# The carried state's product, put on two column tiles of TensorE

## The chip, the cores and the metric

The kernel runs on one core of a Trainium2 chip. The metric is the device time of one execution in microseconds (us); less is better.

## What is computed

Two blocks, one after the other: a gated linear recurrence over 768 steps with a complex decay (4 batches, 8 heads, head size 48), and a feed-forward block with SiLU on its result, 3072 tokens of 384 numbers, 2048 hidden.

```python
mag = np.sqrt(a_re * a_re + a_im * a_im)
scale = np.minimum(mag, 0.999) / (mag + 1e-06)
a_re_n, a_im_n = (a_re * scale, a_im * scale)
for t in range(S):
    new_re = ar * S_re - ai * S_im          # ar, ai: the gates of step t
    new_im = ar * S_im + ai * S_re
    kv = np.einsum('bhd,bhe->bhde', k[:, :, t], v[:, :, t])
    S_re, S_im = (new_re + kv, new_im)
    y[:, :, t] = np.einsum('bhd,bhde->bhe', q[:, :, t], S_re)
x = y.transpose(0, 2, 1, 3).reshape(B * S, H * D)
h = x @ w_in
out = (h / (1 + np.exp(-h))) @ w_out
```

All inputs and outputs are float32 on the device; w_in and w_out come as 64-bit floats and are converted in the kernel.

## The kernel before

**Tiling.** Time is cut into chunks of C = 128 steps: 6 chunks in each of 4 batches, N = 24 in all, taken in pairs (p = 0 to 11). A chunk's complex decay is folded into its keys and queries: from the logarithm of the magnitude and from the angle, both summed over the chunk with one product each (`sums`, L343, tile `L`; `phases`, L322, tile `phase`), come the factors by which `rotated` (L366 to L370) multiplies k and q. The results `kr` and `qr` have, for each head, 2 x 48 = 96 columns (D2), the cosine half and the sine half.

**A chunk's attention.** `turned` puts kr and qr with their 96 columns on partitions (tile `T`; by TensorE, L386, for the first eight chunks, by DVE and DMAs for the others). `weights` (L406, tiles `a` and `w`) multiplies keys and queries of each head, and DVE masks the result (L411). `state` (L455, tile `s` in PSUM, 96 partitions of 8 x 48 numbers) multiplies, for each head, kr as the stationary operand (128 steps x 96 columns) by v as the moving one (128 steps x 48): the chunk's contribution to the carried state. DVE adds the old state and multiplies by the decay (L460 to L463, tile `S`); the next chunk of the same batch, two pairs later, reads it. The last chunk of a batch has no `state`, so it is called 20 times. `output` (L427 from v and `w`, L430 from the state and `T`, tile `y`) writes head pairs: the even head to PSUM partitions from 0 on, the odd one to those from 64 on. ACT copies `y` to `xT` (L436, L440), and small DMAs on SP's queue (L444) move a part of it.

**The feed-forward block.** For a pair of chunks (256 tokens) `hidden` (L473, tile `h`) makes two blocks of 128 hidden units per call, ACT applies SiLU (L243, tile `g`), and `result` (L485, tile `o`) adds their products with w_out. There are eight calls of each for a pair.

**Order.** TensorE's order is written out by hand throughout. From the fourth pair on, all engines' order is: a string names the parts, for the usual pair

```python
usual = ("c h h E kA qA L F h kB h tA G r qB r h tB r th h A X r h r aA pA sA yA h pB aB S r lA "
         "sB yB r lB D r")
```

where `h` and `r` are calls of `hidden` and `result` for the pair before, and `aA pA sA yA` are `weights` of chunk A, `phases` of the next pair, `state` and `output`. A `state` thus stands after `phases` or `sums` and is followed by `output`. Before that, `attend(n)` calls `weights` twice, `state` and `output`. Across the engines, semaphores that the framework sets keep the order; the products of one `state` signal once, after the last of them.

Of the kernel before, what the change touches and what calls it, by code (L numbers as in the profile page):

```python
# [55 lines left out]
def kernel(  # L56
# [19 lines left out]
    nc = tc.nc  # L76
# [6 lines left out]
    D2 = 2 * D  # L83
# [27 lines left out]
    def place(n):  # L111
        p, i = divmod(n, 2)
        c, half = divmod(p, B // 2)
        return 2 * half + i, c
# [333 lines left out]
    def state(n):  # L448

        x = X[n]  # L450
        if place(n)[1] == NCH - 1:
            return
        ps = p_m.tile([D2, H, D], F32, tag="m", name=f"s{n}")
        for h in range(H):
            nc.tensor.matmul(ps[:, h], lhsT=x["kr"][:, h].rearrange("p c d -> p (c d)"),  # L455
                             rhs=x["v"][:, h], start=True, stop=True)
        new = att.tile([D2, H, D], F32, tag="S", name=f"S{n + B}", bufs=5)
        by = decs[:, n].unsqueeze(2).to_broadcast([D2, H, D])
        if "S" in x:
            nc.vector.tensor_tensor(out=new, in0=ps, in1=x["S"], op=ALU.add)  # L460
            nc.vector.tensor_tensor(out=new, in0=new, in1=by, op=ALU.mult)
        else:
            nc.vector.tensor_tensor(out=new, in0=ps, in1=by, op=ALU.mult)  # L463
        X[n + B]["S"] = new
# [34 lines left out]
    def step(p, h, r, order):  # L499
# [3 lines left out]
        if p < NP:  # L503
            what["E"] = lambda: (table("exp"), both(decays, p))
            for i, x in enumerate("AB"):
                n = 2 * p + i
                what["k" + x] = lambda n=n: rotated(n, "k")
                what["q" + x] = lambda n=n: rotated(n, "q")
                what["t" + x] = lambda n=n: turned(n)
                what["a" + x] = lambda n=n: (weights(n, 0), weights(n, 1))  # L510
                what["s" + x] = lambda n=n: state(n)
                what["y" + x] = lambda n=n: output(n)
# [38 lines left out]
    def attend(n):  # L551
        weights(n, 0)
        weights(n, 1)
        state(n)
        output(n)
# [300 lines left out]
```

## Time and profile before

| | |
|---|---|
| time, median of 3 runs (lowest to highest) | 721.26 us (719.17 to 721.49) |
| profiled execution: its time | 722.11 us |
| profiled execution: span from first to last instruction | 720.4 us |
| granted TensorE clock, mean | 0.991 |
| TensorE matmuls, busy | 673.2 us, 3552 passes |
| TensorE weight loads, busy | 512.2 us, 3552 loads |
| VectorE (DVE), ScalarE (ACT) busy | 334.3 us, 362.8 us |

The profile names engines PE (TensorE's matmuls), PEld (its weight loads, which overlap matmuls), DVE, ACT, POOL and SP. A row of the groups reads: line, engine, operation, what is written and read, shapes, how often; then busy time, mean length of one in ns, and the idle time just before, with what ended it. For a matmul the first shape is rows times columns of the array that are in use, the second the moving operand. Ends of matmuls are modelled, since they are pipelined; starts are what distances are taken from. In the forty slices a digit is the busy share of 18 us in tenths.

### The profile page before, as it was taken

What the parts mean: (1) busy time and instruction counts of PE and PEld (TensorE: products, weight loads), DVE (VectorE), ACT (ScalarE), POOL (GpSimd) and SP (SyncE); (2) the same over time, 40 slices, a digit from 0 to 9 for tenths busy, and PEclk for the clock granted to TensorE, in tenths of its full rate; (3) what the DMA queues carried; (4) which work ended last, traced back from release to release, by engine and by line L of the source; (5) the groups of instructions that cost most, each with busy time, mean ns of one, the idle gap of its engine ahead of it and who ended that gap; (6) DMA issues with size and microseconds to landing.
All of it is one profiled execution on the core that took longest, in us unless ns stands there. A gap on an engine that the chain in (4) does not pass through costs nothing.

```text
span 720.4 us, 9485 instructions
## 1 busy us (share of the span) xinstructions
PE 673.2 (93%) x3552; PEld 512.2 (71%) x3552; DVE 334.3 (46%) x542; ACT 362.8 (50%) x597; POOL 59.7 (8%) x91
## 2 busy tenths in 40 slices
PE   0486997999999999999999999999999999999997
PEld 0275875777768778778778778777777777777774
DVE  4989758826443183182282272272272372151000
ACT  7985679548782382381381381381381481231201
POOL 2333001030000010010010010010010010010000
PEclk9998999999999999999999999999999999999999
DMA  9956347110150027128127228127227327023000
GB/s 184 232 133 159 93 135 175 45 45 17 48 97 1 28 41 139 47 34 142 51 37 138 52 34 143 50 33 134 60 29 125 73 27 128 28 40 51 29 1 25
DMA packets 207845, 55.51 MB, mean 77 GB/s; under 512 B 198424, under 2 KB 202672, under 8 KB 207792
## 3 DMA queue, kind: packets, MB, share of 16 engines
q1 hardware_dynamic: 199712, 43.55, 31.5%
q0 software_dynamic: 3584, 6.37, 4.4%
q10 hardware_dynamic: 4496, 4.92, 1.9%
q8 instruction: 30, 0.49, 0.3%
q14 instruction: 23, 0.19, 0.1%
HBM read 36.25 MB, written 4.76 MB: 57 GB/s over the span
## 4 chain that ended last, share of the span: by engine, by line
PE 86%; ACT 5%; DVE 3%; DMA 3%; SPq 2%; issue 1%; ACTq 0%
PE h L473 33%; PE o L485 32%; PE a L406 6%; PE s L455 4%; PE y L427 3%; PE y L430 2%; PE phase L322 2%; PE L L343 2%; PE tp L386 2%; DMA raw<-in_moe_w_in_dram 1%; ACT s L243 1%; ACT L238 1%; DMA q<-in_q_dram 1%; ACT mag L243 1%; SPq L135 1%
## 5 line engine op out<-in xcount | busy, mean ns | idle before, releaser
L473 PE MATMUL h<-xT,w 128*128 128x256 f32 x1152 | 261.2, 382 | 6.2 <-DMA xT<-y 6.2
L485 PE MATMUL o<-w,g 128*128 128x384 f32 x768 | 261.1, 488 | 0.0
L473 PEld LDWEIGHTS h<-xT,w 128*128 128x128 f32 x1152 | 219.5, 191 | 47.6 <-issue 8.1
L485 PEld LDWEIGHTS o<-w,g 128*128 128x128 f32 x768 | 144.2, 190 | 89.0 <-issue 2.2
L243 ACT ACTIVATE g<-h 128x512 f32<-128x512 f32 x96 | 56.3, 596 | 172.5 <-PE h L473 172.2
L411 DVE TENSOR_TENSOR w<-a,upto 128x512 f32<-128x512 f32 x48 | 33.0, 688 | 110.7 <-PE a L406 110.4
L436 ACT COPY xT<-y 128x384 f32<-128x384 f32 x24 | 11.5, 477 | 117.4 <-PE y L430 112.8
L357 POOL DMA_DIRECT2D decs<-ends x48 | 30.1, 633 | 465.1 <-DMA ends<-eq 464.5
L238 ACT ACT_TABLE_LOAD x50 | 64.2, 1283 | 2.2 <-PEq L840 1.3
L366 DVE TENSOR_TENSOR L<-k,L 128x384 f32<-128x384 f32 x24 | 13.3, 554 | 82.2 <-ACT L L243 82.2
L406 PEld LDWEIGHTS a<-T 96*128 96x128 f32 x384 | 46.7, 193 | 6.7 <-DVE w L411 1.0
L406 PE MATMUL a<-T 96*128 96x128 f32 x384 | 47.4, 276 | 0.8 <-DVE w L411 0.8
L322 PE MATMUL phase<-th,upto 128*128 128x384 f32 x48 | 22.0, 557 | 22.0 <-DVE th L301 19.4
L427 PE MATMUL y<-w,v 128*64 128x128 f32 (+1 forms) x384 | 39.6, 281 | 0.0
L346 DVE TENSOR_SCALAR L<-L 128x384 f32<-128x384 f32 x24 | 13.4, 557 | 56.2 <-PE L L343 55.9
L430 PE MATMUL y<-T,S 96*64 96x128 f32 x320 | 34.3, 273 | 0.0
L455 PEld LDWEIGHTS s<-v,kr 128*96 128x96 f32 x320 | 29.9, 165 | 4.9 <-issue 2.2
L324 DVE TENSOR_SCALAR turn<-phase 128x384 f32<-128x384 f32 x24 | 13.3, 556 | 42.3 <-PE phase L322 42.3
L491 ACT COPY ot<-o 128x384 f32<-128x384 f32 x24 | 11.5, 478 | 40.4 <-PE o L485 40.4
L243 ACT ACTIVATE mag<-mag 128x768 f32<-128x768 f32 (+1 forms) x39 | 30.6, 788 | 0.4
L243 ACT ACTIVATE s<-s 128x768 f32<-128x768 f32 (+1 forms) x39 | 30.5, 785 | 0.4
L455 PE MATMUL s<-v,kr 128*96 128x48 f32 x320 | 30.0, 247 | 0.2
(68 smaller groups left out, 617.5 us busy)
## 6 DMA issues: line engine op xcount, KB each, us to landing
T<-sq SPq DMA_DIRECT2D x192, 64.0 KB
raw<-in_moe_w_out_dram SPq DMA_DIRECT2D x16, 384.0 KB
raw<-in_moe_w_in_dram SPq DMA_DIRECT2D x24, 192.0 KB
out_dram<-ot ACTq DMA_DIRECT2D x24, 192.0 KB
re<-in_a_re_dram SPq DMA_DIRECT2D x18, 192.0 KB
k<-in_k_dram SPq DMA_DIRECT2D x18, 192.0 KB
q<-in_q_dram SPq DMA_DIRECT2D x18, 192.0 KB
im<-in_a_im_dram SPq DMA_DIRECT2D x17, 192.0 KB
```

Source lines behind the costliest of these rows:

```text
L238: chain(nc.scalar.preload_act_table_set({"exp": "natural_log_exp_and_others", "trig": "trig_and_small", "silu": "silu_and_others"}[of]))
L243: chain(nc.scalar.activation(out=out, in_=in_, func=func, **kw))
L322: nc.tensor.matmul(ps, lhsT=upto, rhs=th, start=True, stop=True)
L343: nc.tensor.matmul(ps, lhsT=half, rhs=cut(A[p]["l"], i), start=True, stop=True)
L357: nc.gpsimd.dma_start(out=decs[a * D:(a + 1) * D, n], in_=ends[n].rearrange("(h d) -> d h", d=D))
L406: nc.tensor.matmul(ps[:, h], lhsT=x["kT"][:, hh * HH + h], rhs=x["qT"][:, hh * HH + h], start=True, stop=True)
L411: nc.vector.tensor_tensor(out=x["w", hh], in0=ps, in1=upto.unsqueeze(1).to_broadcast([C, HH, C]), op=ALU.mult)
L427: nc.tensor.matmul(to, lhsT=v_[:, cols], rhs=x["w", h // HH][:, h % HH], start=True, stop=not carried)
L430: nc.tensor.matmul(to, lhsT=x["S"].rearrange("p h d -> p (h d)")[:, cols], rhs=x["qT"][:, h], start=False, stop=True)
L455: nc.tensor.matmul(ps[:, h], lhsT=x["kr"][:, h].rearrange("p c d -> p (c d)"), rhs=x["v"][:, h], start=True, stop=True)
L473: nc.tensor.matmul(ps[:, ji], lhsT=w1[:, dc, ts(jp * 2 + ji, C)], rhs=A[p]["xT"][:, dc], start=(dc == 0), stop=(dc == ND - 1))
L485: nc.tensor.matmul(A[p]["o"][m], lhsT=A[p]["g", jp][:, ji, ts(m, C)], rhs=w2[:, j], start=(j == 0), stop=(j == NJ - 1))
```

## The change

The stationary operand of each head's product, 96 columns, is cut in two: columns 0 to 63 and columns 64 to 95. Each part is a product of its own with the same moving operand, and writes its own partitions of the same PSUM tile (0 to 63, 64 to 95). For each head the wide part is issued first, then the narrow one. Nothing else is changed.

```diff
         ps = p_m.tile([D2, H, D], F32, tag="m", name=f"s{n}")
         for h in range(H):
-            nc.tensor.matmul(ps[:, h], lhsT=x["kr"][:, h].rearrange("p c d -> p (c d)"),
-                             rhs=x["v"][:, h], start=True, stop=True)
+
+            for m in (ds(0, 64), ds(64, D2 - 64)):
+                nc.tensor.matmul(ps[m, h], lhsT=x["kr"][:, h].rearrange("p c d -> p (c d)")[:, m],
+                                 rhs=x["v"][:, h], start=True, stop=True)
```

## The prediction

> **What bounds the kernel now.** I read the page first: busy time by engine, the forty slices, the chain that ended last.
>
> ```profile
> PE 673.2 (93%) x3552; PEld 512.2 (71%) x3552; DVE 334.3 (46%) x542; ACT 362.8 (50%) x597; POOL 59.7 (8%) x91
> ...
> PE   0486997999999999999999999999999999999997
> ...
> PE 86%; ACT 5%; DVE 3%; DMA 3%; SPq 2%; issue 1%; ACTq 0%
> PE h L473 33%; PE o L485 32%; PE a L406 6%; PE s L455 4%; PE y L427 3%; PE y L430 2%; PE phase L322 2%; PE L L343 2%; PE tp L386 2%; DMA raw<-in_moe_w_in_dram 1%; ACT s L243 1%; ACT L238 1%; DMA q<-in_q_dram 1%; ACT mag L243 1%; SPq L135 1%
> ```
>
> TensorE is full from slice 8 (126 us) to the end, and 86% of the chain is its work. The line that changes, L455, is 4% of the chain. The chain cut down to 40 to 66 us and to 70 to 90 us shows the four early calls of `state` on it too. So all twenty calls (24 chunks less the last one of each of four batches) lie on the path: a microsecond added to a call is one added to the end. Now the rows of the groups kept apart by shape:
>
> ```profile
> L406 PE MATMUL a<-T 96*128 96x128 f32 x384 | 47.4, 276 | 0.8 <-DVE w L411 0.8
> L427 PE MATMUL y<-w,v 128*64 128x128 f32 x336 | 38.5, 282 | 0.0
> ...
> L455 PE MATMUL s<-v,kr 128*96 128x48 f32 x320 | 30.0, 247 | 0.2
> ...
> L455 PEld LDWEIGHTS s<-v,kr 128*96 128x96 f32 x320 | 29.9, 165 | 4.9 <-issue 2.2 <-DVE w L411 0.6
> ```
>
> "128*96" is rows times columns of the array, "128x48" the moving operand. 320 is 20 calls x 8 heads x 2: each f32 product is two passes, each with its own weight load. The mean of 247 ns is a latency; what counts is the distance between starts, which the timeline of TensorE gives (start, length, group):
>
> ```profile
> 385.70 1.95 PE L406 MATMUL a<-T 96*128 96x128 f32 x16
> 387.49 0.81 PE L322 MATMUL phase<-th,upto 128*128 128x384 f32 x2
> 388.13 1.48 PE L455 MATMUL s<-v,kr 128*96 128x48 f32 x16
> 389.54 0.45 PE L427 MATMUL y<-w,v 128*64 128x128 f32 x4
> 389.81 0.40 PE L430 MATMUL y<-T,S 96*64 96x128 f32 x4
> ...
> 391.51 2.86 PE L473 MATMUL h<-xT,w 128*128 128x256 f32 x12
> ```
>
> From the starts: `phase` 0.64/2 = 0.32 us for a pass of 384 columns, so a pass streams at 384/320 = 1.2 columns per ns; `a` 1.79/16 = 112 ns for 128 columns (107 at that rate); `s` 1.41/16 = 88 ns for 48 columns, which at 1.2 stream in 40. So `s` isn't bound by its streaming but by its loads of 96 columns. `y`, from 389.54 to 391.51, has 32 passes of 128 columns in 1.97 us, 62 ns each, about half of 107: its heads alternate between PSUM partitions 0 and 64, that is between two column tiles, and these run side by side.
>
> What a change between whole-array and tiled work costs is seen at both ends of `y`, in narrow windows of the timeline:
>
> ```profile
> 389.37 0.25 PE L455 MATMUL s<-v,kr 128*96 128x48 f32 x1
> 389.54 0.45 PE L427 MATMUL y<-w,v 128*64 128x128 f32 x4
> ...
> 389.07 0.42 PEld L455 LDWEIGHTS s<-v,kr 128*96 128x96 f32 x4
> 389.54 0.21 PEld L427 LDWEIGHTS y<-w,v 128*64 128x64 f32 x4
> ...
> 391.51 0.30 PEld L473 LDWEIGHTS h<-xT,w 128*128 128x128 f32 x2 [0.19 <-issue]
> ```
>
> Within `s`, loads run ahead of the pass before. At the change they don't: the last load of `s` began at 389.32 (389.07 + 0.42 less its 0.165), is in at 389.40, its pass has streamed at 389.44, and the first load of `y` starts at 389.54, 0.10 us later. On the way out, the last `y` pass starts at about 391.31, has streamed 107 ns later at 391.41, and `h` loads at 391.51, again 0.10 us. The wait is named "issue": no semaphore holds it. So a change of tiling costs about 95 ns after the last column has streamed, and the next load can't be hidden.
>
> **What the Trainium skill says.** (1) "TensorE: Matmul & The Clock Gate", section "LDWEIGHTS (loading the stationary operand)": a load takes the number of its columns divided by 1.2, in ns. 96 columns: 80 ns; the trace's 88 for a load-bound pass agrees. 64 columns are 53, 32 are 27. (2) "TensorEngine Tiling (Array Packing)", section "Key Properties": tiles work independently, in loads and matmuls; the trace agrees (62 ns against 112). (3) Same section: changing the tiling mode, as against the tile, drains TensorE. The 95 ns at both ends of `y` agree for whole array against tiles. (4) Same page, "Available Configurations", lists 128x64 and 128x32 as two modes. No run here shows a change between these two.
>
> **The change, part by part.** It removes 8 products of 96 columns per call and adds 8 of 64 columns at column 0 and 8 of 32 at column 64. Passes and loads of L455 double: 320 to 640 each. No DMA, semaphore wait, buffer or work of another engine is added or moved; `s` is still one PSUM tile that DVE reads after the last pass. `y` needs 64-wide tiles for its last 48-column heads as well, but an output of 32 columns fits the 128x32 mode, so I take it that each head goes 64, 32, and the next head back to 64: 15 changes inside a call.
>
> Price of a 64-column part (two passes), nothing loaded ahead: first load 53 ns, first pass streams to 93; second load in at about 108 (hidden in part under the first pass), second pass streams to 148; drain 95: 243 ns to the next part's load. Of a 32-column part: load 27, pass to 67, second pass to 107; drain 95: 202 ns. A head: 445 ns, against 2 x 85 to 88 now.
>
> A call, from the end of streaming of what is before it to the first load of `y`: now 1.41 us, with no change of mode ahead of it (whole array to whole array) and one after it, which is in the 1.41. Then: 0.095 for the new change into tiles, 8 x 0.445 = 3.56 with the last drain counted in: 3.65 us. Difference 2.24 us, 20 calls: **+44.9 us**. It is costed in full since TensorE has no idle time to take it; ACT, DVE and the queues just move later. ACT waits on `h` for 172.2 us and DVE on `a` for 110.4 us in the view of waits, so neither becomes the bound. DVE's L460, in order behind `s`, comes 2.2 us later relative to the call's start; its result is needed two pairs of chunks on, and the DVE work queued behind it waits for TensorE anyhow.
>
> The unknown is the change 64 to 32. From below: the tiles overlap and the gain is that of the first rival. From above: besides the drain, no load is hidden even inside a part (53+40+53+40+95 and 27+40+27+40+95 = 510 ns a head): 4.18 us a call, +55 us. I take the 95 ns that the trace shows at two other changes.
>
> The profiled execution has a span of 720.4 and a time of 722.11, 0.85 above the median of 721.26. From the median: 721.3 + 44.9 = 766.
>
> **Rivals.**
> *The tiles overlap* (chance 0.15, the other side: faster). If the array lets a 32-column tile run beside a 64-column one, each works at its own loads: 16 of 64 columns at 55 ns (about `y`'s pace) is 0.88, plus 0.095 into tiling, 0.04 last pass, 0.095 out: 1.11 against 1.41 us, 20 x -0.30 = -6: 715 us. It decides as soon as a part may start before its neighbour has streamed out. For it: `y` does just this with two 64-wide tiles, a 48-column one among them. Against: those are one mode.
> *Overlap without gain* (0.14). Loads share one path: 53 + 27 = 80 a pass pair, as now, plus 0.095 into tiling: +2 us, 723. Or instructions can't be issued faster than in `y`, 62 ns a load and pass: 32 x 0.062 + 0.095 = 2.1, +0.67 a call, +13: 734. For it: the trace shows no faster pace.
> *A part waits for its neighbour to stream out, but not for a drain* (0.07): 148 + 107 = 255 a head, 8 x 255 + 190 = 2.23, +0.82 a call, +16: 738.
> *Drain* as priced: 0.64.
>
> **How the numbers follow.** About 0.3% (2 us) is what a measurement here can tell from no change. Faster: 0.15. Within it: the cheap end of overlap without gain, 0.04. Slower: 0.64 + 0.07 + 0.10 = 0.81. The likeliest is 766; its own bounds are 755 (about 10 us cheaper, if 30 ns of each of the 16 drains in a call are hidden) to 778. The range goes down to 723 to take in the slower rivals and leaves out the overlap and a little above: 723 to 778.
>
> **What would show it.** Right: 640 passes at L455 in two shapes, 128*64 and 128*32; the way from the first pass of `s` to the first `y` load at about 3.5 us; loads of `s` in pairs, with some 95 ns of "issue" after each pair has streamed; L455 at about 9% of the chain (4% of 720 is 28 us, and 45 more, of 766); `h`, `o`, `a` and `y` unmoved in pace. Wrong: loads of the two shapes that start some 15 ns apart, as the first two of `y` do in the trace's records (14 ns), and a call shorter than 1.41 us; or an idle TensorE outside L455, which would mean that the delay moved some other order.

## The result, and the profile after

The changed kernel takes 770.34 us (769.74 to 776.51) where the one before took 721.38 in the same comparison: a ratio of 1.0699, interval 1.0637 to 1.0762. The forecast was slower, 766 us, within 723 to 778. The profiled execution has a span of 769.0 us and a time of 770.71, against 720.4 and 722.11.

The page after: busy time, slices with the granted clock, chain.

```profile
PE 720.5 (94%) x3872; PEld 538.8 (70%) x3872; DVE 333.8 (43%) x542; ACT 363.4 (47%) x597; POOL 60.2 (8%) x91
...
PE   0496998999999999999999999999999999999997
...
PEclk9696999999999999999999999999999999999999
...
PE 86%; ACT 5%; DMA 3%; DVE 3%; SPq 2%; issue 1%; ACTq 0%
PE h L475 31%; PE o L487 30%; PE s L457 9%; PE a L406 5%; PE y L427 4%; PE y L430 3%; PE phase L322 2%; PE L L343 2%; PE tp L386 2%; DMA raw<-in_moe_w_in_dram 1%; ACT s L243 1%; ACT L238 1%; ACT mag L243 1%; DMA q<-in_q_dram 1%; SPq L135 1%
```

TensorE is as full as before and its share of the chain the same; the changed line (now L457) went from 4% to 9% of it. It has 320 passes and as many loads more. A full TensorE says nothing on how well it is used: the rows by shape and the timeline do.

The groups of the changed line, kept apart by shape:

```profile
L457 PE MATMUL s<-v,kr 128*64 128x48 f32 x320 | 50.6, 240 | 0.4 <-DVE w L411 0.2
L457 PE MATMUL s<-v,kr 128*32 128x48 f32 x320 | 44.0, 220 | 0.0
...
L457 PEld LDWEIGHTS s<-v,kr 128*64 128x64 f32 x320 | 30.7, 135 | 18.2 <-issue 7.6 <-DVE w L411 1.0
L457 PEld LDWEIGHTS s<-v,kr 128*32 128x32 f32 x320 | 22.1, 108 | 8.7
```

Each single load and pass is shorter than the 96-column ones were (165 and 247 ns), but there are twice as many, and loads sit idle 27 us where it was 4.9. The timeline of one call (start, length, group), first TensorE, then its weight loads in narrow windows:

```profile
415.11 0.81 PE L322 MATMUL phase<-th,upto 128*128 128x384 f32 x2
415.85 3.65 PE L457 MATMUL s<-v,kr 128*64 128x48 f32 x32
419.43 0.70 PE L427 MATMUL y<-w,v 128*64 128x128 f32 x4
```

```profile
415.85 0.19 PEld L457 LDWEIGHTS s<-v,kr 128*64 128x64 f32 x2 [0.55 <-issue]
...
416.10 0.14 PEld L457 LDWEIGHTS s<-v,kr 128*32 128x32 f32 x2
...
416.30 0.19 PEld L457 LDWEIGHTS s<-v,kr 128*64 128x64 f32 x2
...
416.54 0.14 PEld L457 LDWEIGHTS s<-v,kr 128*32 128x32 f32 x2
...
416.75 0.19 PEld L457 LDWEIGHTS s<-v,kr 128*64 128x64 f32 x2
```

From the first pass of `s` to the first of `y` it is 3.58 us now (419.43 - 415.85), 1.41 before. The loads come in pairs, 0.25 us from a wide pair to the narrow one and 0.20 us from there to the next wide one (to the ns in the trace's records: 245 and 202). Reckoned as in the prediction, with 40 ns of streaming for a pass once its load is in, each pair starts to load some 95 ns after the pair before has streamed, so the wide and the narrow tile never run at the same time.

Where the 48.6 us of the span are: from the end of streaming of what precedes `s` to the first load of `y`, the twenty calls together take 45.3 us more (3.67 us each where they don't wait for other engines). Three `y` products, behind the calls numbered 5, 12 and 16 (from 0), take 3.43, 3.55 and 3.45 us in place of 1.96: 4.5 us. The first four calls shift the fifth by 8.1 us and not by 9.1: the work ahead of the first call ended 0.8 us sooner in this execution than in the one before, and the rest was taken up where TensorE waits for DVE and DMAs.

### The profile page after: what moved, and what is told of

The parts are those of the page before. It is cut to its first block, busy times and chain, and to the rows that moved or that the text cites. A ratio compares the mean times of both kernels' runs of the same rounds, so it can differ in the third digit from the quotient of the medians.

```text
span 769.0 us, 10128 instructions
## 1 busy us (share of the span) xinstructions
PE 720.5 (94%) x3872; PEld 538.8 (70%) x3872; DVE 333.8 (43%) x542; ACT 363.4 (47%) x597; POOL 60.2 (8%) x91
## 4 chain that ended last, share of the span: by engine, by line
PE 86%; ACT 5%; DMA 3%; DVE 3%; SPq 2%; issue 1%; ACTq 0%
PE h L475 31%; PE o L487 30%; PE s L457 9%; PE a L406 5%; PE y L427 4%; PE y L430 3%; PE phase L322 2%; PE L L343 2%; PE tp L386 2%; DMA raw<-in_moe_w_in_dram 1%; ACT s L243 1%; ACT L238 1%; ACT mag L243 1%; DMA q<-in_q_dram 1%; SPq L135 1%
## 5 line engine op out<-in xcount | busy, mean ns | idle before, releaser
L457 PE MATMUL s<-v,kr 128*32 128x48 f32 (+1 forms) x640 | 73.5, 230 | 0.4 <-DVE w L411 0.2
L457 PEld LDWEIGHTS s<-v,kr 128*32 128x32 f32 (+1 forms) x640 | 52.8, 122 | 26.9 <-issue 7.6
L427 PE MATMUL y<-w,v 128*64 128x128 f32 (+1 forms) x384 | 43.5, 306 | 0.0
L430 PE MATMUL y<-T,S 96*64 96x128 f32 x320 | 36.7, 291 | 0.0
```

Of the source, the lines that this page charges most:

```text
L427: nc.tensor.matmul(to, lhsT=v_[:, cols], rhs=x["w", h // HH][:, h % HH], start=True, stop=not carried)
L430: nc.tensor.matmul(to, lhsT=x["S"].rearrange("p h d -> p (h d)")[:, cols], rhs=x["qT"][:, h], start=False, stop=True)
L457: nc.tensor.matmul(ps[m, h], lhsT=x["kr"][:, h].rearrange("p c d -> p (c d)")[:, m], rhs=x["v"][:, h], start=True, stop=True)
```

## The experiments

Theory: at each change between the 64 mode and the 32 mode (column tiles 64 or 32 wide) TensorE drains, that is, it starts no load until some 95 ns after the last column has streamed. Rivals: the number of passes, any change of tile, a shared load path. The edits are to the changed kernel. Where a call is said to take so many us, it is from the end of streaming of what precedes `s` to the first load of `y`.

**Grouped: all wide parts, then all narrow ones.** The same 640 passes, 3 changes of mode a call with the way out, not 17.

```diff
-        for h in range(H):
-            for m in (ds(0, 64), ds(64, D2 - 64)):
+        for m in (ds(0, 64), ds(64, D2 - 64)):
+            for h in range(H):
```

> Same 640 passes at the product of the state, but all eight 64-column parts first, then all eight 32-column parts: 2 changes of tiling inside and ahead of a call (with the way out, 3) in place of 16. Theory (a change between the 64 mode and the 32 mode waits for the last column and then 95 ns, and hides no load): 0.095 + (0.053 + 15 x 0.055 + 0.040) + 0.095 + (0.027 + 15 x 0.043 + 0.040) + 0.095 = 1.92 us a call against 3.67 changed and 1.41 before: about 731 us. Rival (the cost is the doubled number of passes and loads, which is the same here): stays at 770.

Measured: 730.13 us (729.3 to 734.89), ratio to the kernel before 1.0145 (1.0113 to 1.0176). The timeline of TensorE:

```profile
390.62 0.81 PE L322 MATMUL phase<-th,upto 128*128 128x384 f32 x2
391.37 1.93 PE L456 MATMUL s<-v,kr 128*64 128x48 f32 x32
393.22 0.45 PE L427 MATMUL y<-w,v 128*64 128x128 f32 x4
```

1.85 us from the first pass of `s` to `y` with the same 32 passes that took 3.58. The number of passes isn't the cost; their order, and with it the number of changes of mode, is.

**Serpentine: neighbours share a mode.** Odd heads do the narrow part first: 9 changes a call.

```diff
+            wide, narrow = ds(0, 64), ds(64, D2 - 64)
-            for m in (ds(0, 64), ds(64, D2 - 64)):
+            for m in ((wide, narrow) if h % 2 == 0 else (narrow, wide)):
```

> Even heads wide then narrow, odd heads narrow then wide, so that two neighbouring parts share a mode: 8 changes inside a call, none at its end (it ends in the 64 mode, as the next product begins). Theory: 0.095 + 0.243 + 4 x 0.290 + 3 x 0.353 + 0.148 = 2.71 us a call: about 747 us, between the grouped order and the changed kernel in step with the number of changes. Rival (number of passes): 770.

Measured: 745.67 us (745.26 to 746.16), ratio 1.0341 (1.0319 to 1.0362). In the trace a call takes 2.69 us, 2.71 expected. With 3, 9 and 17 changes of mode the calls take 1.95, 2.69 and 3.67 us: 122 ns a change. Some 95 of these are the drain; the rest, by the prediction's prices, is a load or a pass that no longer runs beside another.

**One mode: 64 and 48 columns.** The same two positions and the same order by head, but for the last head, which is done first and whole; only the narrow part's width puts it into the 64 mode. (Of the edit, the old loop and DVE's reads of `ps[0:D2]` are left out here.)

```diff
-        ps = p_m.tile([D2, H, D], F32, tag="m", name=f"s{n}")
+        ps = p_m.tile([C, H, D], F32, tag="m", name=f"s{n}")
+        kr = x["kr"].rearrange("p h c d -> p (h c d)")
+        for h in (H - 1, *range(H - 1)):
+            for at, m in ((0, D2),) if h == H - 1 else ((0, 64), (64, 48)):
+                nc.tensor.matmul(ps[at:at + m, h], lhsT=kr[:, ds(h * D2 + at, m)],
+                                 rhs=x["v"][:, h], start=True, stop=True)
```

> The second part reads 48 columns in place of 32 (16 columns of the next head, whose results nobody reads), so that both parts are tiles of the 64 mode; order by head as in the changed kernel, at the same partitions 0 and 64. The last head has no next one: it is done first and whole (96 columns, in the mode of what is before). Theory: no change of mode inside a call, the two tiles run side by side at the wide one's loads, and the next product follows in the same mode without a drain: 0.17 + 0.095 + 0.053 + 13 x 0.055 + 0.04 = 1.07 us against 1.41: about 714.5 us, faster than both. Rival 1 (every change of tile waits, not just of mode): 13 waits, near 760. Rival 2 (loads share one path, 53 + 40 a pass pair): 1.6 us a call, 725.

Measured: 715.57 us (714.93 to 715.72), ratio 0.9919 (0.9903 to 0.9935). The timeline:

```profile
384.03 0.81 PE L322 MATMUL phase<-th,upto 128*128 128x384 f32 x2
384.68 1.24 PE L457 MATMUL s<-v,kr 128*96 128x48 f32 x30
385.75 0.44 PE L427 MATMUL y<-w,v 128*64 128x128 f32 x4
```

1.07 us from the first pass of `s` to `y`, where the 96-column products took 1.41 and the 64 and 32 ones 3.58. This is the run that decides: a wider, in part useless, second part turns the changed version into one faster than the kernel before. So it isn't the tile that waits, nor a load path that both share; it is the mode. The one head left whole doesn't explain it: that alone gives 761.97 us (the run with the first head whole, below). That tiles of one mode go their own way is seen in the first call too: the first pass of `y` starts at 44.60 us, before the last pass of `s` at 44.65 us, which stands ahead of it in the program.

**Three tiles of 32.** One mode again, the other one.

```diff
-            for m in (ds(0, 64), ds(64, D2 - 64)):
+            for m in (ds(0, 32), ds(32, 32), ds(64, 32)):
```

> Three parts of 32 columns at partitions 0, 32 and 64, all of the 32 mode: 960 passes, one change into the mode and one out of it. Theory with three tiles side by side, bound by streaming 48 columns (40 ns, some 43 a pass): 0.095 + 0.027 + 15 x 0.043 + 0.04 + 0.095 = 0.90 us a call: 711 us. Rival 1 (TensorE can't take a load and a pass faster than in the tiled product behind it, some 55 to 62 ns): 48 x 0.055 + 0.19 = 2.8 us, 750. Rival 2 (loads share one path, 27 each): 1.5 us, 723.

Measured: 713.68 us (712.13 to 715.54), ratio 0.9893 (0.9873 to 0.9913). The timeline:

```profile
384.63 0.81 PE L322 MATMUL phase<-th,upto 128*128 128x384 f32 x2
385.37 0.88 PE L457 MATMUL s<-v,kr 128*32 128x48 f32 x48
386.18 0.45 PE L427 MATMUL y<-w,v 128*64 128x128 f32 x4
```

48 passes and loads in 0.81 us, 17 ns each, where one pass alone streams for 40: neither issue nor a shared load path binds, and three tiles stream at once. A call is 0.90 us in the trace, as expected. The time is 2.7 us above the 711 expected. The rows by shape show TensorE waiting for DVE's mask in the early calls, for 3.4 us where the kernel before has 0.8 at `a` and 0.2 at `s`:

```profile
L406 PE MATMUL a<-T 96*128 96x128 f32 x384 | 48.1, 279 | 1.8 <-DVE w L411 1.8
...
L457 PE MATMUL s<-v,kr 128*32 128x48 f32 x960 | 18.2, 211 | 1.6 <-DVE w L411 1.6
```

That is 2.4 us more, about the size of the miss: a shorter `state` is of no use where TensorE then waits for DVE. The profiled execution was the slowest of the five (715.54 us) and has, besides, a stretch of 6.8 us at half clock, a granted clock of 0.5 (166.6 to 173.4 us), over the call numbered 5, which took 1.43 us from first pass to `y` (0.81 in others), with 1.45 us more in the `y` behind it.

**The rest: a clock that halves.** What was still open is the 4 us by which the result lies above the sum, and the three long `y`. Windows of the changed kernel around the call shown above (length, busy time of PE, PEld, DVE, ACT, POOL, granted clock, DMA share, GB/s):

```profile
415.90:419.30 3.40, 3.40 (x33) 2.51 (x32) 1.18 (x3) 0.00 (x0) 0.00 (x0) 1.00 1.01 191
419.30:422.70 3.40, 3.40 (x34) 3.33 (x34) 1.11 (x2) 0.00 (x0) 0.00 (x0) 0.51 1.15 219
422.70:426.10 3.40, 3.40 (x19) 2.72 (x17) 0.00 (x0) 0.81 (x3) 0.00 (x0) 0.99 1.05 191
```

The `y` behind `s` ran at half clock. All stretches of half clock in the trace's record of the clock, but the one that the execution's end cuts off, are whole multiples of 3.413 us, on one grid. I call the calls' parts, with a drain between each two, the drained stretch, and what stands before and behind it dense work: its passes follow each other without drains. Of the 20 calls exactly three, 5, 12 and 16, hold a whole step of that grid in their 3.67 to 3.77 us between dense work, and these three have the slow `y`. (Half clock follows call 1 too, in the start, where a step held 0.14 us of dense work.) The Trainium skill, "TensorE: Matmul & The Clock Gate", section "Part 1: The HAM clock gate", says that a free-running window of 3413 ns in which TensorE is idle halves its clock. The grid agrees; but here the profile shows TensorE busy throughout, only sparsely.

*First head whole, to shorten the drained stretch.*

```diff
-            for m in (ds(0, 64), ds(64, D2 - 64)):
+            for m in (ds(0, 64), ds(64, D2 - 64)) if h else (ds(0, D2),):
```

> The changed kernel with the first head's product left whole (96 columns, before the change into tiles): the stretch of drained parts gets shorter, 0.095 + 7 x 0.4475 = 3.23 us, and so shorter than 3.41 us, the length of the stretches of half clock in the changed kernel's record. Theory on the rest of the loss (the clock is halved for 3.41 us after a stretch of that length that lies wholly in the drained parts; this made three of the y products 1.5 us longer): none such beyond the first 130 us, so 721.3 + 20 x (0.17 + 3.23 - 1.41) - 1 = about 760 us. Rival (y is slower after drained parts for another reason): only 20 x 0.28 less than the changed kernel, 764.7, and y products of 3.4 us remain.

Measured: 761.97 us (761.49 to 763.24), ratio 1.0557 (1.0533 to 1.0581): 2 us over the theory, 2.7 under the rival. One `y` beyond 130 us, at call 16, is slow still (3.47 us), where I had expected none. Its windows:

```profile
527.88:531.29 3.41, 3.41 (x34) 2.52 (x34) 1.26 (x4) 0.00 (x0) 0.00 (x0) 1.00 0.95 186
531.29:534.70 3.41, 3.41 (x33) 3.05 (x29) 0.99 (x2) 0.05 (x1) 0.00 (x0) 0.50 1.06 204
```

This step of the grid ended 0.24 us after the first load of `y`, so it needn't lie in the drained stretch to the last. Three slow products became one, and 1.5 us of the 2 us are that one.

*The changed kernel once more, without an edit.*

> The changed kernel once more, unaltered. Theory: stretches of half clock beyond 130 us come at other calls or in another number, but only at calls in whose drained stretch of 3.67 us one step of a fixed 3.41 us grid lies wholly; each makes the y behind it 1.4 to 1.6 us longer. Rival (it depends on what stands around the call): the calls numbered 5, 12 and 16 again, whatever the grid.

Measured: 768.65 us, one run. The slow `y` were behind calls 5, 12 and 16 again (3.25, 3.42 and 3.36 us), since the grid fell in nearly the same place relative to the calls; this run doesn't tell the theories apart. At call 5 the step began 0.16 us before the end of the work ahead of `s`, at call 16 0.04 us before it, and both halved the clock; at call 19 a step that reached 0.28 us into `y` did not. With the run before, about a quarter of a microsecond of dense work in a step is where it turns in these drained calls. It isn't a general limit: in the run with three tiles of 32, half clock followed a step (163.19 to 166.60 us) that held 1.6 us of dense work and then a wait for DVE, with PE busy for 1.89 us in all; in the changed kernel a step with PE busy for only 1.56 us (129.25 to 132.66 us) was followed by full clock. What is counted stays open.

*Each product twice, to lengthen the drained stretch.*

```diff
-        for h in range(H):
+        for h in (*range(H), *range(H)):
```

> The changed kernel with each state's product made twice (the second overwrites the first with the same numbers): 7.26 us of drained parts a call. Theory with the grid of 3.41 us: every call holds a whole step of it, so every y behind it is slow, and the end of the drained parts too: 837 us for the parts alone, and some 1.4 to 2.5 us more in each of 20 calls: 865 to 890. Rival (no such cause): 837 to 842, with a few slow y products.

Measured: 894.01 us, ratio 1.2382 (1.2346 to 1.2418). One call in the timeline:

```profile
564.18 8.26 PE L457 MATMUL s<-v,kr 128*64 128x48 f32 x64
572.36 0.70 PE L427 MATMUL y<-w,v 128*64 128x128 f32 x4
572.84 0.65 PE L430 MATMUL y<-T,S 96*64 96x128 f32 x4
573.27 0.70 PE L427 MATMUL y<-w,v 128*64 128x128 f32 x4
573.70 0.69 PE L430 MATMUL y<-T,S 96*64 96x128 f32 x4
```

Four passes of `y` in 0.43 us, not 0.22, and in the trace half clock follows every one of the 20 calls: from the fifth on the `y` behind them take 3.63 to 3.67 us, the four `y` of the last chunks, with no `s` ahead, 1.96. So it is the drained stretch that halves the clock. The 4 us above the range that I gave are only in part accounted for: the drained parts slow down too once the clock has halved, to 7.7 to 9.2 us from first pass to `y`, 8.2 in the mean of the 20 calls, in place of 7.2. With 1.7 us for each `y` from the fifth call on (0.9 or less before) that is some 2.6 us a call, just above the 1.4 to 2.5 us of the expectation.

**State and `y` in one mode.** From the three tiles of 32 on, `y` cut to the same mode. (The two products of `y`, now inside the new loop, are left out here.)

```diff
-                cols = ds(h * D, 64 if h + 1 < H else D)
-                to = ps[64 * r:64 * r + (64 if h + 1 < H else D), hp]
+                for c in (0, 32):
+                    w = min(32, width - c)
+                    cols = ds(h * D + c, w)
+                    to = ps[64 * r + c:64 * r + c + w, hp]
```

> Three parts of 32 as in the run with 128*32 tiles alone, and the product behind it, y, in parts of 32 and 16 columns too (672 and 280 passes of its 64-wide tiles become twice as many narrow ones), so that state and y share one mode and no drain stands between them. Theory: 20 x 0.095 = 1.9 us less than 713.7, y at its old pace since four tiles of 32 stream side by side: 711.8. Rival (y's doubled passes cost issue time, at 17 ns a pass as in the 48-pass state or more; or four tiles don't stream at once): y longer than 1.96 us, 714 or more.

Measured: 710.92 us (710.52 to 711.2), ratio 0.9845 (0.9827 to 0.9863), the fastest here. The timeline:

```profile
382.32 0.88 PE L460 MATMUL s<-v,kr 128*32 128x48 f32 x48
383.02 0.44 PE L430 MATMUL y<-w,v 128*32 128x128 f32 x8
...
384.96 1.99 PE L478 MATMUL h<-xT,w 128*128 128x256 f32 x8
```

`y` starts 0.70 us after the first pass of `s`, 0.11 sooner than with the 64-wide `y`, which is the drain; and `y` itself takes 1.94 us (384.96 - 383.02) to the first pass of `h`, with twice the passes, way out included. (The 672 passes in the expectation should be 336: with the 48-wide ones, `y` has 704 passes before and 1408 now.)

## Why the prediction was right

**Twenty calls on the path: right.** The span grew by 48.6 us: the 45.3 us of the calls and the 4.5 us of the slow `y`, less some 1 us in the start.

**A change of mode drains for some 95 ns, also from 64 to 32: right,** the one step that rested on the Trainium skill (points 3 and 4 of the prediction) and not on a trace. A wide part took 245 ns (243 predicted), a narrow one 202 (202), a call 3.67 us (3.65). It was argued from two changes between whole array and tiles; the grouped, serpentine and one-mode runs show it: the cost goes with the number of changes of mode, and with none inside the call it turns into a gain. One reading of the prediction was loose, without consequence: the 88 ns for a pass of 96 columns contain the way out; inside a call four such passes start within 0.34 us (389.03 to 389.37), 85 ns apart.

**The sum: 4 us short.** 44.9 us were forecast for the calls and 45.3 measured; the medians differ by 49.0. The term left out is the clock: three `y` at half clock, 4.5 us. The working took the pace of `y` as unmoved. In the trace before, no drain is longer than 0.1 us, and half clock, but for the end, is recorded only in the first 125 us, where TensorE has idle time (the slices of 18 us, granted clock in tenths):

```profile
PEclk9998999999999999999999999999999999999999
```

I didn't ask whether drained passes would count as idle. That this term stayed small was luck: the drained stretch of 3.67 us is barely longer than a step of 3.41, so that few calls met a whole one. With all 20 met it would have been some 30 us (20 x 1.5, an estimate from the three slow `y`), and the time above 778.

**The rivals.** *The tiles overlap:* the mechanism is real, but for tiles of one mode: the one-mode run gained 5.8 us (721.34 - 715.57), and the rival's number was 6. *Overlap without gain* and *a wait without a drain*: ruled out by the narrow windows above, and the 17 ns a pass of the three tiles show that neither issue nor a shared load path is near.

## What to carry to other kernels

Before a product is cut into column tiles, look at the widths: parts that fall into different modes (here 64 and 32 columns) cost some 120 ns at each change and did not overlap in any run here, while parts of one mode run side by side, even if one has to be padded to get there. Order work so that neighbours share a mode, across products too: state and the product behind it in one mode gave 710.9 us where the kernel before took 721.3. A stretch of drained, sparse passes that is long enough to fill a whole step of the 3.413 us grid costs a second time, in the dense work behind it, which then runs at half clock.

## What the runs showed of the hardware that I had not expected

A TensorE that the profile shows as busy without a break can still lose its clock: passes of 40 ns at a mean distance of 112 ns (four in a head of 447 ns) over one whole step of a 3.413 us grid were enough for 3.4 us or more at half clock, and up to about 0.24 us of dense work inside the step didn't prevent it, while 0.28 us in another did. What the hardware counts in such a step isn't shown. With the serpentine order (2.69 us a call) no half clock was recorded beyond 70 us but at the end.
